# Moving transposes, casts and loads to DMA queues in a linear attention followed by a low-rank mixer

## The chip, the cores and the metric

One core of a Trainium2 chip runs the program. The metric is the device time of one execution in microseconds, the median of several. An engine has its own instruction queue: TensorE (PE), VectorE (DVE), ScalarE (ACT), GpSimd (POOL) and SyncE (SP, here only a queue for DMAs).

## What is computed

Batch 8, 8 heads, 576 positions, head size 64, so a model width of 512. From the reference, shortened:

```python
def phi(x): r = np.maximum(x, 0); return np.concatenate([r * cos_w, r * sin_w], axis=-1)   # 64 -> 128 features
kv = einsum('bhsf,bhsd->bhfd', phi(k), v);  z = phi(k).sum(axis=2)
x  = einsum('bhsf,bhfd->bhsd', phi(q), kv) / (einsum('bhsf,bhf->bhs', phi(q), z) + 1e-6)   # heads side by side: (B, S, 512)
u  = x + (x.transpose(0, 2, 1) @ U @ V).transpose(0, 2, 1)                                  # rank 32, over the positions
out = u + np.maximum(u @ w_ch1, 0) @ w_ch2                                                  # 512 -> 2048 -> 512
```

## The kernel before

A batch's 576 positions are four chunks of 128 (c = 0 to 3) and a tail of 64; the tails of an even and an odd batch share one tile of 128 rows. Attention of a batch: `k_prep` and `q_prep` (L221, L227) make the features in bf16, a cosine half and a sine half per chunk; `v_prep` (L195) casts v on GpSimd; `kv_unit` (L233) sums kv and z for four heads; the q features are transposed, by TensorE against an identity (`qtr_unit`, L254, copied out of PSUM), or by a DMA (`qtr_dma`, L268, used only where BY_DMA holds); `x_unit` (L333) makes one chunk of x. The first batch goes by halves of four heads (`den_unit`, `xh_unit`, L295, L312). Then `A_unit` (L360) makes U^T x, `u_unit` (L376) adds V^T A to one chunk, and u is transposed by `utr_unit` (L399) or `utr_dma` (L414). The first two batches get their transposed u straight from x and A (`uTd_open`, `uTd_close`, L427, L437).

The network runs on pairs of batches, in a list of 72 slots per pair (`mlp_slots`, L591): 16 main slots of the even batch (`g1_main`, L463: four matmuls of 128x512, emptied by ScalarE into `hid`), 16 of the odd one, 4 tail slots, and 36 slots of the second matmul (`g2_part`, four matmuls each; every fourth adds u on VectorE into `o_sb`, which SP stores). The order of all work is written by hand: instructions are issued in program order, and `todo` (L716 to L721) says behind which slot which unit of the next pair's attention stands. `pe_plan` (L554) and `prep_plan` (L581) give the offsets. BY_DMA (L534) is False, so all transposes are TensorE's.

Loads: all of them on SP's queue, but the tails of batch 0, U and V, which ScalarE issues (L126 to L138). The weights come as fp32 into a staging tile with two buffers (`w1_load`, L89), and GpSimd casts them (`w1_cast`, L97). A tile that is asked for again waits until its last reader is done; the number of buffers is `bufs`.

Of the kernel before, what the change touches and what calls it, by code (L numbers as in the profile page):

```python
# [17 lines left out]
def kernel(  # L18
# [13 lines left out]
    B = 8  # L32
# [56 lines left out]
    def w1_load(n):  # L89
        st = pool.tile([P, 4, 512], FP32, tag="wst", bufs=2, name="wst")  # L90
        nc.sync.dma_start(
            out=st,
            in_=moe_w_ch1.rearrange("(d p) n -> p d n", p=P)[:, :, n * 512 : n * 512 + 512],
        )
        return st

    def w1_cast(n, st, eng):  # L97
        cast(eng, w1_bf[:, :, n * 512 : n * 512 + 512], st)

    def w2_load(n):  # L100
        st = pool.tile([P, 4, 512], FP32, tag="wst", bufs=2, name="wst")
        nc.sync.dma_start(
            out=st,
            in_=moe_w_ch2.rearrange("(j p) n -> p j n", p=P)[:, n * 4 : n * 4 + 4, :],
        )
        return st

    def w2_cast(n, st, eng):
        cast(eng, w2_bf[:, n * 4 : n * 4 + 4, :], st)
# [16 lines left out]
    load_tail(kt[0], k, 0, A_)  # L126
    load_tail(qt[0], q, 0, A_)
    load_tail(vt[0], v, 0, A_)
    for h0 in (0, 4):
        load_main(kst[0], k, 0, h0, h0 + 4)  # L130
        load_main(qst[0], q, 0, h0, h0 + 4)
        load_main(vst[0], v, 0, h0, h0 + 4)
    A_.dma_start(
        out=stU[:, 0:4, :], in_=moe_U[0:512, :].rearrange("(p c) r -> p c r", c=4)
    )
    for lo in (0, TS):
        A_.dma_start(out=stU[lo : lo + TS, 4, :], in_=moe_U[512:S, :])
    A_.dma_start(out=stV, in_=moe_V)  # L138

# [19 lines left out]
    make_identity(nc, ident)  # L159

# [17 lines left out]
    G_.memset(U_bf, 0.0)  # L178
    G_.memset(V_bf, 0.0)
# [115 lines left out]
    def den_unit(b, hg, tag, bufs):  # L295
        d_ps = ps.tile([P, 5, 4], FP32, tag=tag, bufs=bufs, name="d_ps")
        for c in range(5):
            for i in range(4):
                h = hg * 4 + i
                nc.tensor.matmul(  # L300
                    out=d_ps[:, c, i : i + 1],
                    lhsT=qT_of(b, c, h),
                    rhs=kv_sb[b][:, h, D:E],
                    start=True,
                    stop=True,
                )
        rec = pool.tile([P, 5, 4], FP32, tag="rec5", bufs=2, name="rec5")
# [4 lines left out]
    def xh_unit(b, c, hg, rec, tag, bufs):  # L312
        x_alloc(b)
        rows = slice(0, P) if c < 4 else tail(b)
        acc = ps.tile([P, 4, D], FP32, tag=tag, bufs=bufs, name="xh_ps")
        for i in range(4):
            h = hg * 4 + i
            nc.tensor.matmul(
                out=acc[:, i, :], lhsT=qT_of(b, c, h), rhs=kv_sb[b][:, h, 0:D],
                start=True, stop=True,  # L320
            )
        nc.vector.tensor_tensor(
            out=x_of(b, c, rows)[:, hg * 256 : hg * 256 + 256].rearrange(
                "p (i d) -> p i d", d=D
            ),
            in0=acc[rows],
            in1=rec[rows, c, :].unsqueeze(2).to_broadcast(
                [P if c < 4 else TS, 4, D]
            ),
# [224 lines left out]
    def pe_plan(b):  # L554

        plan = []
        if BY_DMA:
            plan.append((-4, lambda: qtr_dma(b, 4, 5)))
            plan.append((-2, lambda: qtr_dma(b, 0, 2)))
            plan.append((0, lambda: qtr_dma(b, 2, 4)))  # L560
        else:
            for c in range(5):
                plan.append((2 * c, lambda c=c: qtr_unit(b, c)))
        for hg in range(2):
            plan.append((1 + 2 * hg, lambda hg=hg: kv_unit(b, hg, "X", 1)))
        for c in range(5):
            plan.append((5 + 2 * c + (2 if c == 4 else 0), lambda c=c: x_unit(b, c, "X", 1)))
        tx = "T" if BY_DMA else "X"
        plan.append((18, lambda: A_unit(b, tx, 1)))
        for n, c in enumerate((4, 0, 1, 2, 3)):  # L570
            plan.append((21 + 2 * n, lambda c=c: u_unit(b, c, tx, 1)))
            if not BY_DMA and c < 4:
                plan.append((24 + 2 * n, lambda c=c: utr_unit(b, c)))
        if b % 2 == 1:
            plan.append((23, lambda: utr_dma(b, 4, 5) if BY_DMA else utr_unit(b, 4)))
        if BY_DMA:
            plan.append((27, lambda: utr_dma(b, 0, 2)))
            plan.append((31, lambda: utr_dma(b, 2, 4)))
        return plan

    def prep_plan(b):  # L581

        plan = [(0, lambda: v_prep(b))]
        for n, c in enumerate((4, 0, 1, 2, 3)):
            plan.append((n, lambda c=c: k_prep(b, c, (V_, V_))))
            for i in range(2):
                engs = (A_, None) if i == 0 else (None, A_)
                plan.append(((n if BY_DMA else 3 + 2 * n) + i, lambda c=c, e=engs: q_prep(b, c, e)))
        return plan

    def mlp_slots(pr):  # L591
        e, o = 2 * pr, 2 * pr + 1
        slots = [lambda j=j: g1_main(e, j) for j in range(NJ)]
        slots += [lambda j=j: g1_main(o, j) for j in range(NJ)]
        slots += [lambda j=j: g1_tail(pr, j) for j in range(4)]
        slots += [
            lambda cc=cc, p=p: g2_part(pr, cc, p) for cc in range(9) for p in range(4)
        ]
        return slots
# [48 lines left out]
    w2st = {0: w2_load(0), 1: w2_load(1)}


    first = {}

    def at(j, *thunks):
        first.setdefault(j, []).extend(thunks)

    for n, c in enumerate(ORD):
        at(n // 2, lambda c=c: k_prep(1, c, (V_, A_)))
        at(4 + n // 2, lambda c=c: q_prep(1, c, (V_, A_)))
    for n, c in enumerate(ORD):
        at(1 + n // 2, lambda c=c: u_unit(0, c, "o", 2))  # L660
    for n, c in enumerate(ORD):
# [90 lines left out]
```

## Time and profile before

| | |
|---|---|
| median of 3 runs | 375.38 us (375.27 to 375.92) |
| profiled execution | 376.63 us, its span 374.5 us |
| mean granted TensorE clock | 0.991 |
| busy: TensorE, VectorE, ScalarE, GpSimd | 332.6, 180.9, 147.9, 44.5 us |
| moved by DMA | 46.68 MB, mean 125 GB/s |

The profile is one execution. Busy time of TensorE is modelled: a matmul's duration reaches into its neighbours', so its pace is read from start to start. In a row, "<-" in brackets names what ended the idle time before it.

### The profile page before, as it was taken

How to read it: one execution, taken by the hardware profiler on the slowest of the kernel's cores; microseconds unless marked ns; L12 is line 12 of the kernel's file. 1: busy time of each engine (PE TensorE's matmuls, PEld its weight loads, DVE VectorE, ACT ScalarE, POOL GpSimd, SP SyncE). 2: the span in 40 equal slices, each digit the busy share in tenths (PEclk: the TensorE clock that was granted, in tenths of full speed). 3: DMA queues.
4: the chain of work that ended last, by engine and by line, in shares of the span. 5: the costliest groups of instructions: out<-in, count | busy, mean ns of one | idle time of the engine just before them, and what ended most of it. 6: DMA issues, size and time to landing. Idle time of an engine off the chain costs nothing.

```text
span 374.5 us, 6199 instructions
## 1 busy us (share of the span) xinstructions
PE 332.6 (89%) x2589; PEld 183.1 (49%) x2589; DVE 180.9 (48%) x389; ACT 147.9 (39%) x254; POOL 44.5 (12%) x70
## 2 busy tenths in 40 slices
PE   0358787999989899999989999999899999999995
PEld 0356244446635534654755445544665444455442
DVE  3273865483676696543647483534565450000221
ACT  0861681369620420455671502455730006662000
POOL 2443642340000203030000003000000000000000
PEclk9999898999999999999999999999999999999999
DMA  8999889900329559900005278000012110000212
GB/s 210 308 299 329 290 279 283 291 17 16 114 77 292 152 163 291 275 19 2 0 30 169 72 229 263 2 0 2 0 39 76 56 58 28 0 2 28 86 56 84
DMA packets 47531, 46.68 MB, mean 125 GB/s; under 512 B 14064, under 2 KB 38768, under 8 KB 47504
## 3 DMA queue, kind: packets, MB, share of 16 engines
q1 hardware_dynamic: 45568, 45.75, 41.3%
q10 hardware_dynamic: 1936, 0.55, 0.7%
q8 instruction: 20, 0.33, 0.4%
q14 instruction: 7, 0.06, 0.0%
HBM read 36.86 MB, written 9.44 MB: 124 GB/s over the span
## 4 chain that ended last, share of the span: by engine, by line
PE 73%; DVE 14%; ACT 5%; issue 3%; DMA 3%; POOL 1%; ACTq 1%; POOLq 0%; DVEq 0%
PE o_ps L511 27%; PE g_ps L468 26%; PE t_ps L258 4%; DVE k_p L209 4%; PE kv_ps L241 3%; PE gt_ps L486 3%; DMA st_uv<-in_moe_U_dram 3%; PE x_ps L340 3%; PE a_ps L366 2%; ACT q_p L207 2%; PE va_ps L383 2%; DVE o_sb L522 2%; DVE u_bf L384 1%; PE t_ps L409 1%; DVE x_bf L350 1%
## 5 line engine op out<-in xcount | busy, mean ns | idle before, releaser
L475 ACT ACTIVATE hid<-g_ps 128x512 bf16<-128x512 f32 x128 | 76.3, 596 | 128.6 <-PE g_ps L468 128.6
L468 PE MATMUL g_ps<-uT,w_bf 128*128 128x512 bf16 x512 | 123.9, 385 | 0.1
L511 PE MATMUL o_ps<-w_bf,hid 128*128 128x512 bf16 x512 | 121.4, 379 | 0.0
L468 PEld LDWEIGHTS <-w_bf 128*128 128x128 bf16 x512 | 48.4, 99 | 53.7 <-issue 5.0
L511 PEld LDWEIGHTS <-hid 128*128 128x128 bf16 x512 | 47.7, 98 | 51.7 <-issue 2.9
L522 DVE TENSOR_TENSOR o_sb<-u_bf,o_ps 128x512 f32<-128x512 bf16 x32 | 21.9, 684 | 65.4 <-PE o_ps L511 65.1
L199 POOL CAST v_ext<-vst 128x512 bf16<-128x512 f32 (+1 forms) x36 | 19.2, 575 | 154.8 <-DMA vst<-in_v_dram 132.2
L115 DVE COPY q_pT<-t_ps 128x1024 bf16<-128x1024 bf16 x26 | 17.9, 689 | 20.4 <-PE t_ps L258 20.4
L384 DVE TENSOR_TENSOR u_bf<-x_bf,va_ps 128x512 bf16<-128x512 bf16 x32 | 21.7, 681 | 12.1 <-PE va_ps L383 11.9
L258 PE MATMUL t_ps<-ident,q_p 128*128 128x128 bf16 x256 | 21.0, 230 | 3.9 <-ACT q_p L207 3.3
L258 PEld LDWEIGHTS <-q_p 128*128 128x128 bf16 x256 | 17.7, 103 | 11.5 <-ACT q_p L207 5.6
L207 ACT ACTIVATE q_p<-qst,sinw 128x512 bf16<-128x512 f32 (+1 forms) x36 | 23.2, 662 | 0.0
L258 PE MATMUL t_ps<-ident,q_tl 128*128 128x128 bf16 x64 | 5.5, 229 | 18.8 <-ACT q_tl L207 15.1
L350 DVE TENSOR_TENSOR x_bf<-x_ps,rec 128x512 bf16<-128x512 f32 x28 | 19.4, 691 | 1.0
L383 PE MATMUL va_ps<-A_sb,V_bf 128*128 128x512 bf16 x40 | 15.2, 384 | 4.5 <-DVE u_bf L384 2.3
L209 DVE TENSOR_SCALAR k_p<-kst,cosw 128x512 bf16<-128x512 f32 (+1 forms) x36 | 18.8, 539 | 0.1
L207 ACT ACTIVATE q_p<-qst,cosw 128x512 bf16<-128x512 f32 x24 | 17.0, 710 | 1.5 <-DMA qst<-in_q_dram 1.4
L207 ACT ACTIVATE q_tl<-qt,cosw 64x512 bf16<-64x512 f32 x6 | 4.3, 717 | 32.7 <-PE t_ps L258 22.1
L115 POOL CAST w_bf<-wst 128x2048 bf16<-128x2048 f32 x8 | 15.5, 1934 | 14.4 <-DMA wst<-in_moe_w_ch_dram 14.4
L292 DVE TENSOR_SCALAR rec<-x_ps 128x8 f32<-128x8 f32 (+1 forms) x35 | 5.8, 165 | 20.9 <-PE x_ps L340 20.7
L340 PEld LDWEIGHTS <-q_pT 128*128 128x128 bf16 x224 | 10.5, 100 | 10.2 <-DVE x_bf L350 4.0
L486 PE MATMUL gt_ps<-uT_tl,w_bf 128*128 128x128 bf16 x256 | 15.4, 219 | 0.0
(88 smaller groups left out, 294.6 us busy)
## 6 DMA issues: line engine op xcount, KB each, us to landing
wst<-in_moe_w_ch_dram SPq DMA_DIRECT2D x8, 1024.0 KB, 6.9
out_dram<-o_sb SPq DMA_DIRECT2D x32, 256.0 KB, 2.4
kst<-in_k_dram SPq DMA_DIRECT2D x7, 1024.0 KB, 9.2
qst<-in_q_dram SPq DMA_DIRECT2D x7, 1024.0 KB, 7.2
vst<-in_v_dram SPq DMA_DIRECT2D x7, 1024.0 KB, 9.2
kst<-in_k_dram SPq DMA_DIRECT2D x2, 512.0 KB, 7.9
qst<-in_q_dram SPq DMA_DIRECT2D x2, 512.0 KB, 6.6
vst<-in_v_dram SPq DMA_DIRECT2D x2, 512.0 KB, 6.4
```

Source lines behind the costliest of these rows:

```text
L115: eng.tensor_copy(out=o, in_=i)
L207: nc.scalar.activation(out=o, in_=i, func=AF.Relu, bias=0.0, scale=w)
L209: eng.tensor_scalar(out=o, in0=i, scalar1=0.0, scalar2=w, op0=ALU.max, op1=ALU.mult)
L258: nc.tensor.transpose(out=t_ps[:, h, :], in_=q_p[b][:, c, h, :] if c < 4 else q_tl[:, h, :], identity=ident,)
L350: nc.vector.tensor_tensor(out=x_of(b, c, rows).rearrange("p (g i d) -> p g i d", g=2, d=D), in0=view[:, :, :, 0:D], in1=rec[rows].unsqueez ...
L383: nc.tensor.matmul(out=va, lhsT=V_bf[:, c, :], rhs=A_sb[b], start=True, stop=True)
L384: nc.vector.tensor_tensor(out=u_bf[b][:, c, :] if c < 4 else u_tl[b // 2][rows, :], in0=x_of(b, c, rows), in1=va[rows, :], op=ALU.add,)
L468: nc.tensor.matmul(out=g_ps.rearrange("p (c t) -> p c t", c=4), lhsT=w1_bf[:, d, j * P : j * P + P], rhs=uT[b][:, :, d, :], start=(d == 0) ...
L475: nc.scalar.activation(out=hid[b][:, j, :], in_=g_ps, func=AF.Relu, bias=0.0, scale=1.0)
L486: nc.tensor.matmul(out=g_ps[:, jj, :], lhsT=w1_bf[:, d, j * P : j * P + P], rhs=uT_tl[pr][:, d, :], start=(d == 0), stop=(d == 3),)
L511: nc.tensor.matmul(out=o, lhsT=lhs[:, j, c * P : c * P + P], rhs=w2_bf[:, j, :], start=(j == 0), stop=(j == NJ - 1),)
L522: nc.vector.tensor_tensor(out=o_sb, in0=u, in1=o, op=ALU.add)
```

## The change

- Weights: `w1_load` and `w2_load` become DMAs on GpSimd's queue that read fp32 and write bf16; the staging tiles and GpSimd's casts go. The eight are issued in the start, five of them behind `v_prep(1)`.
- Loads: batch 0 (without tails) and batch 1 stay on SP; the tails of batch 0, U and V, and all loads of batches 2 to 7 go to GpSimd's queue. ScalarE issues no DMA.
- For batches 2 to 7 the q features and u are transposed by DMAs on SP (one for the tail, two for two chunks each); `attention_plan` takes the place of `pe_plan` and `prep_plan`, over one list of 288 slots. Batch b starts at w = 34, 50, 106, 122, 178, 194; batch 2's and 3's network starts at slots 72 and 88, and so on.
- `qst`, `qt` and `x_bf` get a second buffer. Batch 1 uses `den_unit` and `xh_unit` over eight heads; the u units of batch 0 move behind slot 17; the order of the start changes.

The core of the diff:

```diff
     def w1_load(n):
-        st = pool.tile([P, 4, 512], FP32, tag="wst", bufs=2, name="wst")
-        nc.sync.dma_start(
-            out=st,
...
+        cs = slice(n * 512, n * 512 + 512)
+        nc.gpsimd.dma_start(
+            out=w1_bf[:, :, cs], in_=moe_w_ch1.rearrange("(d p) n -> p d n", p=P)[:, :, cs]
+        )
...
-    load_tail(kt[0], k, 0, A_)
...
+    load_tail(kt[0], k, 0, G_)
...
-    BY_DMA = False
...
+    def attention_plan(b):
+        plan = [(-6, lambda: v_prep(b))]
+        for n, c in enumerate(ORD):
+            plan.append((-6 + n, lambda c=c: k_prep(b, c, (V_, V_))))
+            plan.append((-6 + n, lambda c=c: q_prep(b, c, (A_, None))))
+            plan.append((-5 + n, lambda c=c: q_prep(b, c, (None, A_))))
+        plan.append((-3, lambda: qtr_dma(b, 4, 5)))
+        plan.append((-1, lambda: qtr_dma(b, 0, 2)))
+        plan.append((1, lambda: qtr_dma(b, 2, 4)))
+        plan.append((0, lambda: kv_unit(b, 0, "T", 1)))
+        plan.append((2, lambda: kv_unit(b, 1, "T", 1)))
+        for n, c in enumerate(ORD):
+            plan.append((6 + 2 * n, lambda c=c: x_unit(b, c, "X", 1)))
+        plan.append((16, lambda: A_unit(b, "T", 1)))
+        for n, c in enumerate(ORD):
+            plan.append((18 + 2 * n, lambda c=c: u_unit(b, c, "T", 1)))
         if b % 2 == 1:
+            plan.append((20, lambda: utr_dma(b, 4, 5)))
+        plan.append((24, lambda: utr_dma(b, 0, 2)))
+        plan.append((28, lambda: utr_dma(b, 2, 4)))
+        if b + 1 < B:
+            for at, t in zip((-5, -2, 2), loads(b + 1, G_)):
+                plan.append((at, t))
         return plan
...
+    v_prep(0, 4, 8, ORD, (G_, A_, G_, A_, G_))
+    w1_load(0)
+    w1_load(1)
+    l1[1]()
...
+    for n in range(4):
+        w2_load(n)
```

ORD is (4, 0, 1, 2, 3), 4 the tail; V_, A_ and G_ are VectorE, ScalarE and GpSimd.

## Rows read from the trace of the kernel before

**Rows 1.** The page: its busy times, and the chain that ended last by engine.
```profile
PE 332.6 (89%) x2589; PEld 183.1 (49%) x2589; DVE 180.9 (48%) x389; ACT 147.9 (39%) x254; POOL 44.5 (12%) x70
...
PE 73%; DVE 14%; ACT 5%; issue 3%; DMA 3%; POOL 1%; ACTq 1%; POOLq 0%; DVEq 0%
```

**Rows 2.** Windows: stage, its length, busy us (instructions) per engine, TensorE clock, DMA, GB/s.
```profile
12.10:38.20 26.10, 17.13 (x191) 13.91 (x192) 13.28 (x42) 14.15 (x33) 12.53 (x24) 1.00 1.04 317
38.20:75.10 36.90, 30.00 (x236) 15.41 (x235) 23.48 (x41) 19.06 (x32) 14.24 (x11) 0.91 0.97 284
75.10:147.90 72.80, 66.41 (x565) 36.59 (x564) 49.94 (x108) 29.19 (x49) 9.40 (x15) 1.00 0.48 134
147.90:228.30 80.40, 78.41 (x636) 43.55 (x634) 43.85 (x94) 34.28 (x56) 4.61 (x9) 1.00 0.40 115
228.30:308.10 79.80, 78.28 (x634) 43.57 (x633) 40.45 (x84) 27.94 (x46) 1.46 (x3) 1.00 0.14 44
```

**Rows 3.** Timeline of TensorE in pair 1: start, us, instruction.
```profile
148.78 0.61 PE L258 MATMUL t_ps<-ident,q_p 128*128 128x128 bf16 x8
149.23 1.03 PE L468 MATMUL g_ps<-uT,w_bf 128*128 128x512 bf16 x4
150.09 0.28 PE L241 MATMUL kv_ps<-v_ext,k_p 128*128 128x65 bf16 x4
...
150.70 1.03 PE L468 MATMUL g_ps<-uT,w_bf 128*128 128x512 bf16 x4
...
155.65 0.42 PE L340 MATMUL x_ps<-kv,q_pT 128*128 128x65 bf16 x8
155.91 1.02 PE L468 MATMUL g_ps<-uT,w_bf 128*128 128x512 bf16 x4
```

**Rows 4.** Groups by form in 228 to 308 us: busy, mean ns, idle time before.
```profile
L258 PE MATMUL t_ps<-ident,q_p 128*128 128x128 bf16 x64 | 4.9, 219 | 1.5 <-ACT q_p L207 1.5
```

**Rows 5.** Timeline of ScalarE in pair 0.
```profile
83.01 0.71 ACT L207 ACTIVATE q_tl<-qt,sinw 64x512 bf16<-64x512 f32 x1
83.62 0.58 ACT L475 ACTIVATE hid<-g_ps 128x512 bf16<-128x512 f32 x1
84.10 0.71 ACT L207 ACTIVATE q_p<-qst,cosw 128x512 bf16<-128x512 f32 x1
```

**Rows 6.** Timeline of the start, all engines.
```profile
0.73 0.44 SPq L75 DMA_DIRECT2D kst<-in_k_dram  x1
...
10.37 1.28 ACT L155 ACT_TABLE_LOAD   x1 [10.37 <-DMA qt<-in_q_dram]
...
12.36 1.18 DVE L209 TENSOR_SCALAR k_p<-kst,cosw 128x256 bf16<-128x256 f32 x4
...
19.74 1.96 POOL L115 CAST w_bf<-wst 128x2048 bf16<-128x2048 f32 x1
...
19.86 2.77 DVE L209 TENSOR_SCALAR k_p<-kst,cosw 128x256 bf16<-128x256 f32 x4
```

**Rows 7.** Line 209 on VectorE in 38 to 76 us: ns min, median, max.
```profile
L209 DVE TENSOR_SCALAR k_p<-kst,cosw x4: 471/484/2119, 40.2 to 44.2; 128x512 bf16<-128x512 f32 x4
```

**Rows 8.** DMA issues, us to landing: first 13 us; last two lines 148 to 228.
```profile
kst<-in_k_dram SPq DMA_DIRECT2D x2, 512.0 KB, 7.9
qst<-in_q_dram SPq DMA_DIRECT2D x2, 512.0 KB, 6.6
vst<-in_v_dram SPq DMA_DIRECT2D x2, 512.0 KB, 6.4
wst<-in_moe_w_ch_dram SPq DMA_DIRECT2D x1, 1024.0 KB, 6.9
...
st_uv<-in_moe_U_dram ACTq DMA_DIRECT2D x1, 64.0 KB, 10.1
...
out_dram<-o_sb SPq DMA_DIRECT2D x7, 256.0 KB, 2.3
kt<-in_k_dram SPq DMA_DIRECT2D x2, 128.0 KB, 5.0
```

More of the change, by code (lines that the diff above doesn't have):

```diff
@@ L125 @@
     alloc_v(0)
-    load_tail(kt[0], k, 0, A_)
[L127 to L138, printed above, removed]
     iota = const.tile([P, 5], FP32)
@@ L149 @@
         )
+    for h0 in (0, 4):
+        load_main(kst[0], k, 0, h0, h0 + 4)
+        load_main(qst[0], q, 0, h0, h0 + 4)
+        load_main(vst[0], v, 0, h0, h0 + 4)
+    load_tail(kt[0], k, 0, G_)
+    load_tail(qt[0], q, 0, G_)
+    load_tail(vt[0], v, 0, G_)
     halfpi = const.tile([P, 1], FP32)
@@ L159 @@
     make_identity(nc, ident)
+    G_.dma_start(
+        out=stU[:, 0:4, :], in_=moe_U[0:512, :].rearrange("(p c) r -> p c r", c=4)
+    )
+    for lo in (0, TS):
+        G_.dma_start(out=stU[lo : lo + TS, 4, :], in_=moe_U[512:S, :])
+    G_.dma_start(out=stV, in_=moe_V)
     k_tl = const.tile([P, H, 2 * D], BF16)
@@ L193, with v_prep @@
     u_bf, u_tl, uT, uT_tl = {}, {}, {}, {}
-    def v_prep(b, h0=0, h1=H, cs=range(5)):
+    def v_prep(b, h0=0, h1=H, cs=range(5), engs=None):
         vx = v_ext[b % 2]
-        for c in cs:
+        for n, c in enumerate(cs):
+            eng = engs[n] if engs else G_
             if c < 4:
-                nc.gpsimd.tensor_copy(out=vx[:, c, h0:h1, 0:D], in_=vst[b][:, h0:h1, c, :])
+                cast(eng, vx[:, c, h0:h1, 0:D], vst[b][:, h0:h1, c, :])
             else:
-                nc.gpsimd.tensor_copy(
-                    out=vx[tail(b), 4, h0:h1, 0:D], in_=vt[b][tail(b), h0:h1, :]
-                )
+                cast(eng, vx[tail(b), 4, h0:h1, 0:D], vt[b][tail(b), h0:h1, :])
     def scaled_relu(eng, o, i, w):
@@ L293, in recip, with den_unit @@
         nc.vector.reciprocal(out=rec, in_=rec)
-    def den_unit(b, hg, tag, bufs):
-        d_ps = ps.tile([P, 5, 4], FP32, tag=tag, bufs=bufs, name="d_ps")
+    def den_unit(b, h0, h1, tag, bufs):
+        n = h1 - h0
+        d_ps = ps.tile([P, 5, n], FP32, tag=tag, bufs=bufs, name="d_ps")
         for c in range(5):
-            for i in range(4):
-                h = hg * 4 + i
+            for h in range(h0, h1):
                 nc.tensor.matmul(
-                    out=d_ps[:, c, i : i + 1],
+                    out=d_ps[:, c, h - h0 : h - h0 + 1],
                     lhsT=qT_of(b, c, h),
@@ L310, in den_unit, with xh_unit @@
         return rec
-    def xh_unit(b, c, hg, rec, tag, bufs):
+    def xh_unit(b, c, h0, h1, rec, tag, bufs):
         x_alloc(b)
+        n = h1 - h0
         rows = slice(0, P) if c < 4 else tail(b)
-        acc = ps.tile([P, 4, D], FP32, tag=tag, bufs=bufs, name="xh_ps")
-        for i in range(4):
-            h = hg * 4 + i
+        acc = ps.tile([P, n, D], FP32, tag=tag, bufs=bufs, name="xh_ps")
+        for h in range(h0, h1):
             nc.tensor.matmul(
-                out=acc[:, i, :], lhsT=qT_of(b, c, h), rhs=kv_sb[b][:, h, 0:D],
+                out=acc[:, h - h0, :], lhsT=qT_of(b, c, h), rhs=kv_sb[b][:, h, 0:D],
                 start=True, stop=True,
@@ L548, in qq @@
             alloc_q(b)
-            load_tail(qt[b], q, b)
-            load_main(qst[b], q, b)
+            load_tail(qt[b], q, b, eng)
+            load_main(qst[b], q, b, eng=eng)
         return kk, vv, qq
[L554 to L573, printed above, removed]
-        if b % 2 == 1:
[L575 to L578, printed above, removed]
-        return plan
@@ L581, in prep_plan @@
[L581 to L599, printed above, removed]
@@ L630 @@
     a0 = A_unit(0, "X", 1, A_, 0, 256)
-    for c in ORD:
-        xh_unit(0, c, 1, rec1, "o", 2)
+    for c in ORD[:4]:
+        xh_unit(0, c, 4, 8, rec1, "o", 2)
     for d in range(2):
@@ L653, in at @@
+    for n in range(4):
+        w2_load(n)
+    beside = {}
     def at(j, *thunks):
-        first.setdefault(j, []).extend(thunks)
+        beside.setdefault(j, []).extend(thunks)
     for n, c in enumerate(ORD):
[L657 to L661, printed above, removed]
+        at((0, 0, 1, 1, 2)[n], lambda c=c: k_prep(1, c, (V_, A_)))
+        at((3, 4, 5, 6, 7)[n], lambda c=c: q_prep(1, c, (V_, A_)))
@@ new lines @@
+    at(13, lambda: A_unit(1, "T", 1))
+    at(13, lambda: uTd_close(1, 0, V_), lambda: uTd_close(1, 1, V_))
+    at(14, lambda: uTd_open(1, 2, "o", 2), lambda: uTd_open(1, 3, "X", 1))
+    at(14, lambda: uTd_close(1, 2, V_), lambda: uTd_close(1, 3, V_))
+    slots, todo = [], {}
+    for pr in range(NPAIR):
+        e, o = 2 * pr, 2 * pr + 1
+        slots += [lambda j=j, e=e: g1_main(e, j) for j in range(NJ)]
+        slots += [lambda j=j, o=o: g1_main(o, j) for j in range(NJ)]
+        slots += [lambda j=j, pr=pr: g1_tail(pr, j) for j in range(4)]
+        slots += [
+            lambda cc=cc, p=p, pr=pr: g2_part(pr, cc, p) for cc in range(9) for p in range(4)
+        ]
@@ new lines, with put @@
+    for j, ts_ in beside.items():
+        todo[j] = list(ts_)
+    def put(at, thunk):
+        todo.setdefault(at, []).append(thunk)
+    put(17, lambda: uTt_direct(0, "o", 2, V_))
+    for n, (b, c) in enumerate([(b, c) for b in range(2) for c in ORD]):
+        put(18 + n, lambda b=b, c=c: u_unit(b, c, "T", 1))
+    for n, t in enumerate(loads(2, G_)):
+        put(16 + n, t)
+    for b, w in ((2, 34), (3, 50), (4, 106), (5, 122), (6, 178), (7, 194)):
+        for o, t in attention_plan(b):
+            put(w + o, t)
@@ L725 @@
+    for i, s in enumerate(slots):
+        s()
+        for t in todo.get(i, []):
+            t()
 _INS = ['q', 'k', 'v', 'moe_U', 'moe_V', 'moe_w_ch1', 'moe_w_ch2']
```

145 lines of the change are left out of this document (42 added, 103 removed).

## The prediction

> **What bounds the kernel now.** I read the page first: TensorE is busy 89% of the span, and the chain of work that ended last lies on it for 73% [rows 1]. That is a mean over unlike stages, so I cut the span where the work changes [rows 2]: behind the wait for the first data (12.1 us) come the attention of batch 0 (to 38.2), the 16 main slots of batch 0 with the attention of batch 1 woven in (to 75.1), the rest of pair 0 (to 147.9), pairs 1 and 2; pair 3 has no attention beside it. Pairs 1 and 2 leave TensorE idle for 2.0 and 1.5 us of 80: there, what leaves TensorE leaves the time. The start and slots 0 to 15 are different: 17 us busy of 26 and 30 of 37, so waits for VectorE, ScalarE and data set the end. Next I read the pace of TensorE, from one start to the next, since a matmul's own duration overlaps its neighbour [rows 3]: a slot of four matmuls takes 0.86 us, eight transposes of q features 0.45, a kv unit 0.61, an x unit 0.26. From these follow the units not shown: four transposes of u take half of eight, 0.22; a u unit is one 512-wide matmul, 0.86 / 4 = 0.215; an A unit five, 1.08.
>
> **Transposes leave TensorE.** Batches 2 to 7 have five q units (0.45) each, and per pair nine u units (0.22): 10 x 0.45 + 9 x 0.22 = 6.5 us per pair, of three pairs 19.5 us. Their copies on VectorE go too; it is busy for 44 and 40 us of these 80, no bound, so nothing is counted for them.
> In pairs 1 and 2 all of the 6.5 us is on the path. The one wait of weight there, 1.5 us for the q features [rows 4], gets a successor: q features of an even batch are now made in the last four main slots and in the tail slots, where ScalarE also empties every slot. Its pace was 0.61 us for a feature half and 0.48 for a slot [rows 5]; two halves and a slot make 1.7 us against 0.86 of TensorE, over eight slots ScalarE needs 8 x 0.48 + 10 x 0.61 = 9.9 us, TensorE 7.0, and three buffers hide about 1.5 of the 2.9. So 1.4 replaces 1.5: **-6.5 for pair 1, -6.5 for pair 2**.
> In pair 0 behind slot 15 the window is 72.8 us with TensorE busy for 66.4 [rows 2]. Minus 6.5; five more u units come here from the slots before, +1.1; of the 6.4 idle, much is transposes, copies and x units queued on VectorE, and I leave 2.5 of it: -3.9. **-9.3**. Pair 3 has no attention: 0.
>
> **The start.** ScalarE issues seven DMAs and is held at them: its table load begins at 10.37 us and VectorE's main features, which need cosw, start at 12.36 [rows 6]. Without issues the table is there at about 3 us, and the data are late next: the first half of k, issued at 0.73, with the median of 7.9 us to land of such halves [rows 6, 8], is there at 8.6: -3.7. On the second half, four VectorE features took 2.77 us beside a weight cast on GpSimd and 1.18 without [rows 6]; those casts are gone: -1.6. Two half-size casts of v move to ScalarE, between half and the whole of 0.61 each: +1.0. **-4.3**. The tails now go through GpSimd's queue and k's is used first; no DMA of that queue is in the trace. From one side it is as quick as a store (2.3 us), from the other as slow as U in this stage, 10.1 [rows 8]: issued at about 1.3 us, it is there between 3.6 and 11.4. With the 8.6 of k as the later one, the wait shrinks by 1 to 3.7 us.
>
> **Slots 0 to 15.** Now 36.9 us. The weight casts go, beside which VectorE features of 0.48 us took up to 2.12 [rows 7]; the u units move behind. To slot 8 ScalarE is the longest: 9 x 0.48 + 10 feature halves x 0.61 [rows 5] + 3 copies of two slots' size, 3 x 0.96 = 13.3. Then TensorE: 7 slots x 0.86 + kv 1.2 + 40 narrow denominator matmuls at the kv unit's 0.61 / 20 (1.2) + x 1.3 + A 1.1 + four uT groups at 0.22 + 0.215 (1.7) = 12.5, and nothing covers the last A copy and four uT copies on VectorE, taken as 0.8 of a slot each: 3.5. Together 29.3, say 29.6: **-7.3**. Bounds: 0 (the same chain in a new order) and -12 (TensorE's work alone).
>
> **Weights and loads on GpSimd's queue.** Nothing of a casting DMA is in the trace. Lower bound: the weight load's 6.9 us per MB [rows 8], eight in some 55 us; upper: double. The first is needed at 34 us, the last four at some 85 (34 + 30 + 20 slots). Counted at 0: that cover is about 30 us long, if queue and cast keep the pace of SP. Loads on GpSimd stand behind five casts of v and go out 8 slots or more before their use; this cover is thinnest for q between an even and an odd batch. On SP an issue took 0.44 us [rows 6]; on GpSimd I bound it from above by the length of a weight cast there, 1.96 [rows 6]: six issues a batch and five casts of v (counted like a feature half, 0.6) then take 15 us of the 15 that 16 slots last, just full. Counted at 0.
>
> **DMA transposes.** No such transfer is in the trace. Per batch: one of 128 KB, two of 512 KB for q features; two of 256 KB for u (and per pair one tail); all on SP, where the output stores queue behind one that waits. Stores have three buffers, 12 slots, as cover. The x unit of chunk 2 runs 13 slots behind the first large one's place: 13 x 0.86 + kv 1.2 + three x units 0.8 = 13.2 us. For u the slack is 10 slots, 8.6 us, for 256 KB. From below, 256 KB in 2.3 us (the stores), so 4.6 per 512 KB; from above, rows cut into short pieces, as U's 64 KB in 128-byte pieces, 10.1 us, or kt's 128 KB in 256-byte pieces, 5.0 us, that is 20 per 512 KB [rows 8]. I take the halves of k, q and v, the same 512 KB in 1 KB pieces beside other loads: 7.9, 6.6 and 6.4, mean 7.0. Two behind one another: 14.0 against 13.2, a stall of 0.8 us in each of six batches: **+4.8**.
> [...]
>
> **Sum.** -4.3 - 7.3 - 9.3 - 6.5 - 6.5 + 4.8 = -29.1 us. The profiled execution took 376.63 us (span 374.5 and 2.1 around it), the median of the runs is 375.38, 1.25 less: 375.4 - 29.1 = 346.3, say **346.5 us**.
>
> **Rivals.**
> *Slow transposes (ends slower).* If 512 KB hold the queue for t us, each of six batches stalls 2t - 13.2. The other gains are 33.9 us, so the turning point is t = 9.4. At the pace of kt, t = 20: 6 x 26.8 = 161, less 33.9: about 502 us; at t = 10.5 it is 388. For it: features are read across partitions, unlike any row here, and the loads of the next batch go out in the same slots, 3.4 MB that at 284 GB/s [rows 2] fill the DMA engines for 12 us. Against it: each partition's row is long (4 KB), and the DMA engines are used for only 0.40 and 0.14 of pairs 1 and 2 [rows 2]. Chance 0.16. [...]
> *Late weights (ends slower).* If casting DMAs take twice 6.9 us, eight need 110 us from about 17 on, and the second half of the network, due at 85, stands some 40 us: 346 + 40 = 386. For it: VectorE and GpSimd do get into each other's way [rows 7]. Against it: GpSimd is busy for 1.5 to 14.2 us of a stage [rows 2], and its weight casts go. Chance 0.04. [...]
> *Only the transposes pay.* The start and slots 0 to 15 keep their time because the new queue feeds them no faster: 346.5 + 4.3 + 7.3 = 358. Chance 0.22; with stalls of 2 us rather than 0.8 per batch it reaches 365, inside the same case.
> *Everything hides.* No stall at the transposes, and the bounds of the start reached: 337 to 340. Chance 0.10.
>
> **How the numbers follow.** Forecast (340 to 353) 0.46, everything hides 0.10, only the transposes pay 0.22: faster 0.78. No change (0.2% is 0.75 us, about what a measurement of this kernel can tell) needs the gains to be just eaten: 0.02. Slower 0.20. The range runs from 338, just above the best case, to 380: it takes in the forecast, the smaller gain and stalls up to t near 9.8, and leaves out the far ends of the slower cases and of the best. The faster cases' own range is 338 to 366.
>
> **What would show it.** Right: pairs 1 and 2 at about 74 us each, with no transposes on TensorE; each x unit for chunks 0 and 2 waiting under 1 us for its transpose; the first feature before 9 us and the first main slot near 34; slots 0 to 15 in about 30. Wrong: DMA transposes longer than 9.4 us per 512 KB, read as TensorE's waits in front of the x units; main slots that wait for a weight DMA; features that wait for GpSimd's loads; output stores late behind SP's waits.

## The result and the profile after

The changed kernel takes **362.97 us** (median of 4 runs, 361.68 to 366.36) against 375.65 us (4 runs, 375.27 to 377.04) for the kernel before on the same chip: ratio 0.967, 95% interval 0.960 to 0.974. It is faster, by 12.7 us, where 29 were forecast. The profiled execution took 362.37 us, its span 360.6.

The page of the changed kernel, answering to [rows 1] (busy times; its GpSimd queue with packets, MB and share of 16 engines; the chain by engine):

```profile
PE 316.4 (88%) x2281; PEld 164.8 (46%) x2281; DVE 148.1 (41%) x328; ACT 146.5 (41%) x256; POOL 66.8 (19%) x109
...
q0 software_dynamic: 10256, 25.98, 28.0%
...
PE 65%; DMA 14%; ACT 9%; DVE 8%; issue 2%; POOL 0%; SPq 0%; ACTq 0%; DVEq 0%; POOLq 0%
```

TensorE lost 308 matmul instructions and 16 us of busy time, but DMA rose from 3% to 14% of the chain. Where that is, the windows of the same kernel by stage tell (columns as in [rows 2]; start, slots 0 to 15, rest of pair 0, pairs 1 and 2):

```profile
0.00:31.40 31.40, 16.03 (x190) 13.03 (x191) 16.16 (x55) 16.43 (x38) 13.58 (x34) 1.00 1.05 251
31.40:63.50 32.10, 25.69 (x250) 14.16 (x249) 14.95 (x29) 18.17 (x29) 10.70 (x15) 0.95 0.95 192
63.50:136.50 73.00, 64.21 (x473) 32.72 (x472) 40.06 (x83) 24.17 (x41) 27.04 (x38) 0.95 0.88 230
136.50:217.40 80.90, 74.56 (x518) 37.52 (x517) 34.11 (x75) 33.12 (x56) 15.47 (x22) 0.98 0.65 162
217.40:293.20 75.80, 72.76 (x517) 36.93 (x516) 33.84 (x75) 33.12 (x56) 0.00 (x0) 1.00 0.36 79
```

In pair 1 TensorE is now idle for 6.3 us of 80.9 and GpSimd works in the stage (its loads); in pair 2, with the same attention but no GpSimd instruction, it is idle for 3.0 of 75.8. Transposes left both stages; only pair 2 became shorter, by 4.0 us. What TensorE waited for behind slot 15, in the list of waits (us in total, times, longest; a larger row, 13.7 us for ScalarE's q features, lies in the start and in slots 0 to 15):

```profile
PE x_ps L324 <- DMA q_pT<-q_p: 9.8, 3, 5.2
PE kv_ps L229 <- DVE A_sb L105: 2.4, 3, 0.8
PE kv_ps L229 <- DVE u_tl L368: 2.3, 3, 0.8
PE gt_ps L470 <- ACT hid L459: 2.0, 3, 0.7
```

The first line replaces the 1.5 us of [rows 4]: x units stand for a transpose by DMA in batches 2, 3 and 5. The longest, on TensorE's timeline:

```profile
95.13 1.89 PE L495 MATMUL o_ps<-w_bf,hid 128*128 128x512 bf16 x8
102.17 0.62 PE L324 MATMUL x_ps<-kv,q_pT 128*128 128x65 bf16 x8 [5.16 <-DMA q_pT<-q_p]
102.60 3.60 PE L495 MATMUL o_ps<-w_bf,hid 128*128 128x512 bf16 x8
106.00 0.65 PE L324 MATMUL x_ps<-kv,q_pT 128*128 128x65 bf16 x8
```

The eight matmuls before the wait go from 95.13 to the wait's start in 1.9 us; the eight behind it need 3.4 (102.60 to 106.00). Windows around it (the number before the last two is the granted clock) say why: at the end of the wait TensorE is granted 0.50; it works at that level past 104 us and has 1.00 back at 108.

```profile
101.00:102.00 1.00, 0.00 (x0) 0.00 (x0) 0.00 (x0) 0.00 (x0) 0.14 (x1) 0.50 1.22 354
104.00:106.00 2.00, 2.00 (x7) 0.62 (x6) 2.00 (x5) 2.00 (x5) 0.00 (x0) 0.50 0.05 14
108.00:110.00 2.00, 1.97 (x10) 0.69 (x7) 0.60 (x2) 0.00 (x0) 1.10 (x2) 1.00 0.84 157
```

The timelines of SP and GpSimd show what went out together. SP issues batch 2's transposes; GpSimd's loads of batch 4, written for later slots, follow as soon as GpSimd is through with its casts of v and their buffers are free:

```profile
83.97 5.45 SPq L259 DMA_TRANSPOSE q_pT<-q_p  x2
...
190.86 10.55 SPq L259 DMA_TRANSPOSE q_pT<-q_p  x1
```

```profile
85.83 0.90 POOL L75 DMA_DIRECT2D kst<-in_k_dram  x1 [0.35 <-DVE kv L105]
87.40 0.89 POOL L75 DMA_DIRECT2D vst<-in_v_dram  x1
88.96 0.89 POOL L75 DMA_DIRECT2D qst<-in_q_dram  x1
```

The same happens at 190.86 (a single issue takes SP 10.55 us there). From issue to landing, by the view of the tile and by the list of DMAs (median us):

```profile
DMA to landing us min/median/max: 4.3/5.7/15.0
```

```profile
q_pT<-q_p SPq DMA_TRANSPOSE x12, 5.7
uT<-u_bf SPq DMA_TRANSPOSE x12, 3.1
w_bf<-in_moe_w_ch_dram POOLq DMA_DIRECT2D x8, 512.0 KB, 11.0
qst<-in_q_dram POOLq DMA_DIRECT2D x6, 1024.0 KB, 12.6
```

### The profile page after: what moved, and what is told of

Its sections match the earlier page's. It is cut to its first block, busy times and chain, and to the rows that moved or that the text cites. A ratio compares the mean times of both kernels' runs of the same rounds, so it can differ in the third digit from the quotient of the medians.

```text
span 360.6 us, 5601 instructions
## 1 busy us (share of the span) xinstructions
PE 316.4 (88%) x2281; PEld 164.8 (46%) x2281; DVE 148.1 (41%) x328; ACT 146.5 (41%) x256; POOL 66.8 (19%) x109
## 3 DMA queue, kind: packets, MB, share of 16 engines
q1 hardware_dynamic: 55648, 26.75, 32.1%
## 4 chain that ended last, share of the span: by engine, by line
PE 65%; DMA 14%; ACT 9%; DVE 8%; issue 2%; POOL 0%; SPq 0%; ACTq 0%; DVEq 0%; POOLq 0%
PE g_ps L452 27%; PE o_ps L495 25%; DMA q_pT<-q_p 12%; ACT q_p L195 4%; DMA qt<-in_q_dram 2%; PE a_ps L350 2%; PE va_ps L367 2%; DVE k_p L197 2%; PE kv_ps L229 2%; PE gt_ps L470 2%; PE x_ps L324 2%; ACT hid L459 1%; PE t_ps L246 1%; ACT k_p L195 1%; DVE x_bf L310 1%
## 5 line engine op out<-in xcount | busy, mean ns | idle before, releaser
L452 PE MATMUL g_ps<-uT,w_bf 128*128 128x512 bf16 x512 | 117.7, 382 | 0.2
L452 PEld LDWEIGHTS <-w_bf 128*128 128x128 bf16 x512 | 49.9, 98 | 59.9 <-issue 3.5
L105 DVE CAST kv<-kv_ps 128x260 bf16<-128x260 f32 x16 | 6.8, 428 | 64.0 <-PE kv_ps L229 64.0
L324 PE MATMUL x_ps<-kv,q_pT 128*128 128x65 bf16 x192 | 10.8, 200 | 10.6 <-DMA q_pT<-q_p 9.8
L229 PE MATMUL kv_ps<-v_ext,k_p 128*128 128x65 bf16 x256 | 12.9, 199 | 4.9 <-DVE A_sb L105 2.4
L470 PEld LDWEIGHTS <-w_bf 128*128 128x128 bf16 x256 | 15.1, 98 | 4.0 <-issue 2.3
L334 DVE TENSOR_TENSOR x_bf<-x_ps,rec 128x512 bf16<-128x512 f32 x24 | 16.6, 691 | 0.8
L197 DVE TENSOR_SCALAR k_p<-kst,cosw 128x512 bf16<-128x512 f32 (+1 forms) x36 | 15.9, 462 | 1.7 <-DMA kst<-in_k_dram 1.5
L229 PEld LDWEIGHTS <-k_p 128*128 128x128 bf16 x256 | 11.8, 102 | 8.3 <-DVE A_sb L105 3.9
L495 PE MATMUL o_ps<-w_bf,hid_tl 128*128 128x512 bf16 x64 | 15.4, 379 | 0.0
L246 PE MATMUL t_ps<-ident,q_tl 128*128 128x128 bf16 x16 | 2.0, 276 | 13.7 <-ACT q_tl L195 13.7
```

The costliest lines, as they stand in the source:

```text
L105: eng.tensor_copy(out=o, in_=i)
L197: eng.tensor_scalar(out=o, in0=i, scalar1=0.0, scalar2=w, op0=ALU.max, op1=ALU.mult)
L229: nc.tensor.matmul(out=acc[:, i, :], lhsT=k_p[b][:, c, h, :] if c < 4 else k_tl[:, h, :], rhs=vx[:, c, h, :], start=(c == 0), stop=(c == 4),)
L324: nc.tensor.matmul(out=acc[:, g, i * E : i * E + E], lhsT=qT_of(b, c, h), rhs=kv_sb[b][:, h, :], start=True, stop=True,)
L452: nc.tensor.matmul(out=g_ps.rearrange("p (c t) -> p c t", c=4), lhsT=w1_bf[:, d, j * P : j * P + P], rhs=uT[b][:, :, d, :], start=(d == 0) ...
L470: nc.tensor.matmul(out=g_ps[:, jj, :], lhsT=w1_bf[:, d, j * P : j * P + P], rhs=uT_tl[pr][:, d, :], start=(d == 0), stop=(d == 3),)
```

## The experiments

Stages are cut at the starts of ScalarE's first emptied slot of each part (the `hid` rows), so they are comparable between kernels; spans in us.

| kernel | start | slots 0-15 | rest of pair 0 | pair 1 | pair 2 | pair 3 | span |
|---|---|---|---|---|---|---|---|
| before | 39.5 | 34.7 | 74.8 | 80.4 | 79.8 | 65.3 | 374.5 |
| after | 32.8 | 31.8 | 72.9 | 80.9 | 75.9 | 66.3 | 360.6 |
| e1, loads left out | 33.4 | 31.5 | 64.7 | 75.9 | 75.9 | 66.3 | 347.7 |
| e2, kv tag | 33.4 | 32.0 | 78.4 | 82.3 | 74.3 | 66.3 | 366.7 |
| e3, TensorE transposes | 31.7 | 31.7 | 73.0 | 84.4 | 84.2 | 67.5 | 372.7 |
| e4, before with DMA transposes | 40.0 | 34.6 | 75.8 | 84.6 | 83.4 | 65.2 | 383.6 |
| e5, loads moved | 33.5 | 31.5 | 64.7 | 75.9 | 75.9 | 66.5 | 348.0 |
| e6, e5 and kv tag | 33.0 | 31.9 | 63.1 | 74.3 | 74.3 | 66.5 | 343.0 |
| e7, e5 and q earlier | 32.7 | 27.8 | 64.7 | 75.9 | 75.9 | 66.5 | 343.5 |
| e8, before, ScalarE issues none | 37.7 | 32.5 | 74.4 | 80.4 | 79.8 | 65.4 | 370.1 |
| e9, loads on SP | 32.5 | 31.9 | 64.7 | 75.9 | 75.9 | 66.7 | 347.7 |
| e10, e6 and q earlier | 32.6 | 27.8 | 63.1 | 74.3 | 74.3 | 66.5 | 338.6 |
| e12, loads on ScalarE | 32.7 | 31.6 | 72.5 | 83.6 | 83.1 | 66.3 | 369.9 |
| e13, moved loads on ScalarE | 32.0 | 31.7 | 64.7 | 81.1 | 79.9 | 66.5 | 356.0 |

**Theory:** loads that run beside the DMA transposes slow them. **Rival:** the transposes are slow by themselves, or come too late in the list of slots.

### e1: without the loads of batches 4 to 7

```diff
+            if b >= 4:
+                kst[b], kt[b] = kst[b - 2], kt[b - 2]
+                return
```

(and the like for v and q)

> The changed kernel without the loads of batches 4 to 7 (all but v's tails): these batches read the staging tiles of batches 2 and 3 again, so the output is not the reference's. Collision theory (the DMA transposes of batches 2, 3 and 5 are late, up to 15 us, because GpSimd's queue sends the next loads in the same microseconds): the three waits of TensorE for q_pT (5.2, 1.4 and 3.3 us) and the two stretches at the halved clock behind them go, 12 to 14 us, so about 349 to 351 us, with every DMA transpose of 512 KB landing in 4 to 7 us. Rival (the transposes are slow by themselves, or are held on SP by the stores before them): they stay late and the time stays at 361 to 364.

Measured: 349.12 us (348.88 to 349.45), ratio to before 0.930 (0.925 to 0.934). No wait for q_pT, and

```profile
DMA to landing us min/median/max: 4.2/4.5/6.4
```

So the collisions cost 362.97 - 349.12 = 13.9 us, all of it in the rest of pair 0 and in pair 1: 9.8 of idle TensorE, and about 4 for the slow clock behind two of the waits (an estimate from the granted clock: 5.4 and 3.4 us of work at half speed). Without these loads 512 KB take 4.5 us in the median.

### e2: kv units in the other PSUM buffers

```diff
-        plan.append((0, lambda: kv_unit(b, 0, "T", 1)))
+        plan.append((0, lambda: kv_unit(b, 0, "X", 1)))
```

(and the second kv unit likewise; T and X are buffers of PSUM: the kv matmuls write them and VectorE's 16 casts read kv_ps out of them, 0.43 us each in the changed kernel)

> The changed kernel with the kv units of batches 2 to 7 in the PSUM buffer X in place of T. Theory: the kv units of the odd batch wait behind A and u units of the even batch for their VectorE copies, 0.79 and 0.77 us a pair, in three pairs: 4.7 us less, about 358; the two waits in front of the kv units are gone from the trace. Rival (these waits lie beside another that ends later, the transposes, which then start no later and are waited for instead): less than 1.5 us gained, above 361.

A miss: 367.12 us (364.88 to 368.51), ratio 0.977 (0.972 to 0.983), 4 us slower than the changed kernel, though the ranges of the two overlap. The kv waits went, and pair 2, which has no loads, gained 1.6 us; but with less slack ahead (the time between a transpose's issue and the x unit that needs it) TensorE waited longer still for the transposes, as the rival had it:

```profile
PE x_ps L324 <- DMA q_pT<-q_p: 19.3, 3, 7.0
```

### e3: TensorE's transposes in the changed kernel

```diff
-        plan.append((-3, lambda: qtr_dma(b, 4, 5)))
...
+        for c, o in zip(ORD, (-3, -1, 0, 1, 3)):
+            plan.append((o, lambda c=c: qtr_unit(b, c, eng=V_, tag="X")))
...
+        for c in range(4):
+            plan.append((23 + 2 * c, lambda c=c: utr_unit(b, c)))
```

> The changed kernel with TensorE's transposes in place of the DMA transposes for batches 2 to 7; casting weights, GpSimd's queue and the new order stay. Theory (the DMA transposes take 19.5 us of TensorE's work away and give 13 to 14 back as waits and low clock): 363 + 6 = 369, with pairs 1 and 2 near 80 us and no wait for q_pT. Rival (they give back more than they take): below 362. Second rival (they gain all they were meant to, and the loss is elsewhere): 382.

A miss, half way between the theory's 369 and the second rival's 382: 375.46 us (374.03 to 376.9, 10 runs), ratio 1.001 (0.998 to 1.003). The start and slots 0 to 15 keep their gain of 10.8 us (39.5 + 34.7 against 31.7 + 31.7), and pairs 1 and 2 lose 8.4 of it, pair 3 2.3: TensorE waits in the new order for VectorE between transposes.

```profile
PE t_ps L246 <- DVE x_bf L334: 6.6, 6, 2.5
PE x_ps L324 <- DVE q_tlT L105: 2.8, 3, 0.9
```

So in this order a pair's transposes by DMA are worth 84.4 - 75.9 = 8.5 us where nothing collides, 12.5 us in all as the change has it. Part of this is the run's own: its q transposes stand in the buffer X, which the x units use too, and the two rows come to 3.1 us a pair.

### e4: DMA transposes in the kernel before

```diff
-    BY_DMA = False
+    BY_DMA = True
```

> The kernel before with its flag BY_DMA set: the same DMA transposes alone, with all loads on SP's queue in front of and behind them and 2 to 3 slots less slack. Collision theory: loads and transposes stand in one queue, a transpose behind a 1 MB load waits 4 us and more and the slack is 6 to 9 us, so some stalls stay: 362 to 372, and the waits for q_pT are found where a load was issued just before. Rival (only GpSimd's queue, which runs ahead of the slots, makes the collisions): 19.5 less, about 356.

A miss: 384.91 us (383.69 to 385.43), ratio 1.025 (1.020 to 1.029). The transposes land soon after their issue, yet TensorE waits longer for them than in the changed kernel:

```profile
DMA to landing us min/median/max: 4.3/4.7/7.2
```

```profile
PE x_ps L340 <- DMA q_pT<-q_p: 24.1, 5, 8.1
```

They are issued too late. Batch 3's q features are ready at 104.2 us, but on SP its transposes stand behind stores, loads and a transpose of u; TensorE begins to wait at 119.8, before the first one of 512 KB goes out (timelines of SP and TensorE):

```profile
121.10 3.56 SPq L271 DMA_TRANSPOSE q_pT<-q_p  x1
...
126.67 0.62 PE L340 MATMUL x_ps<-kv,q_pT 128*128 128x65 bf16 x8 [6.89 <-DMA q_pT<-q_p]
```

So it goes with three of the four long waits. The theory's mechanism, one queue for loads and transposes, is among the causes, though the time is far above its 372; no run separates the place in the list from what stands ahead on SP. The change needs the slack too: at 4.7 us a transfer, a late issue costs more than the transposes save.

### e5: the loads out of the way of the transposes

```diff
-        if b + 1 < B:
+        if b == 2:
             for at, t in zip((-5, -2, 2), loads(b + 1, G_)):
...
+        ev, od = loads(2 * p + 2, nc.sync), loads(2 * p + 3, nc.sync)
+        v_odd = loads(2 * p + 3, G_)[1]
+        for at, t in zip((-7, -6, 7, 8, 9, 32), (ev[0], ev[1], ev[2], od[0], od[2], v_odd)):
+            put(72 * p + at, t)
```

> The changed kernel, complete, with the loads of batches 4 to 7 at other times: k and v of the even batch at slots -7 and -6 of its pair's predecessor, its q and the odd batch's k and q at slots 7 to 9, all on SP's queue (so that they go out in slot time, when no features are transposed); v of the odd batch stays on GpSimd's queue. Collision theory: what counts is that loads and transposes don't fall together, so nearly all of the 13.9 us of the run without loads comes back although every byte is loaded: 349 to 352, no wait for q_pT. Rival (the loads' bytes themselves cost that time, wherever they stand, since the DMA engines are short in all of pairs 0 and 1): above 357.

349.75 us (349.24 to 349.91), ratio 0.931 (0.926 to 0.936), no wait for q_pT: all of e1's gain, with every byte loaded.

```profile
DMA to landing us min/median/max: 4.3/4.5/5.4
```

### e9, e12, e13: which queue, and when

Three runs tell apart what "beside" is. First the loads at the changed kernel's own slots, on SP's queue:

```diff
-            for at, t in zip((-5, -2, 2), loads(b + 1, G_)):
+            for at, t in zip((-5, -2, 2), loads(b + 1, nc.sync)):
```

> The changed kernel with the loads of batches 3 to 7 at their written slots, but on SP's queue in place of GpSimd's. Theory (transposes suffer wherever loads stand in front of or beside them): on SP the k and v loads go out in slot time, just before the transposes, and those stand behind 2.3 MB: waits for q_pT in nearly every batch, 362 or more. Rival (only GpSimd's queue, running ahead of the slots, makes them collide): 350 to 353.

Theory missed: 349.92 us (349.42 to 350.43), ratio 0.930 (0.923 to 0.937), no wait for q_pT. Here the load of q that stands behind the transposes on SP is issued behind them, at 92.63 us, after SP is through with them (SP's timeline, last row). The first transpose of a batch, behind v's load, is slower for it, up to 9.5 us, but inside its slack:

```profile
82.52 0.57 SPq L75 DMA_DIRECT2D vst<-in_v_dram  x1
83.80 7.98 SPq L259 DMA_TRANSPOSE q_pT<-q_p  x2
...
92.63 0.58 SPq L75 DMA_DIRECT2D qst<-in_q_dram  x1
```

```profile
DMA to landing us min/median/max: 4.3/4.6/9.5
```

That left two readings: GpSimd runs ahead of the slots, or a second queue is enough. ScalarE keeps the slots' pace and has its own queue (in this run's page 17.70 MB go over q10, SP's 26.75 over q1; `nc.scalar` for `G_` in the same line):

> The changed kernel with the loads of batches 3 to 7 at the same written slots, issued by ScalarE instead of GpSimd. ScalarE reaches a slot when its own work there is done, so its queue keeps the pace of the slots, but its ring is another than SP's, on which the transposes go. Theory (what makes loads and transposes collide is that GpSimd reaches the issues long before their slots): about as with the loads on SP, 350 to 354 us, the q transposes landing in a median under 5 us with no wait of TensorE for q_pT, less some 0.6 us of ScalarE's time for each of 30 issues where ScalarE is close to setting the pace (the loads stand in tail slots of the even batches). Rival (two queues side by side share the DMA engines, whatever the slot): 358 to 364 us, landings of 6 us and more in the median, and waits for q_pT as in the changed kernel.

The theory missed again: 373.98 us (371.69 to 376.36, 10 runs), ratio 1.000 (0.997 to 1.003), slower even than the rival's figure. It is not that GpSimd runs ahead. Transposes and loads collide in all three pairs, because the loads now keep to their slots (GpSimd had sent batch 7's before pair 2 began):

```profile
DMA to landing us min/median/max: 4.4/8.9/14.6
```

```profile
PE x_ps L324 <- DMA q_pT<-q_p: 16.3, 4, 5.6
```

ScalarE's issues are not the cause here: TensorE waits for `hid` no longer than in the changed kernel, 2.0 us.

Last, e5's loads, which stand away from the q transposes, on ScalarE's queue:

```diff
+        ev, od = loads(2 * p + 2, nc.scalar), loads(2 * p + 3, nc.scalar)
```

> The kernel with the moved loads, its loads of batches 4 to 7 issued by ScalarE at the same slots (the odd batch's v stays on GpSimd, as there). No load then goes out in the 15 us ahead of a q transpose, but the loads have a queue of their own again. Theory (it is the time that loads and transposes spend on the DMA engines side by side from two queues; apart in time, a second queue does no harm): 349 to 352 us, pairs 1 and 2 at 76 us, q transposes landing in a median of 4.5 us, no wait of TensorE for q_pT. Rival (a second hardware queue with loads slows the transposes for good, or ScalarE's issues hold up its own work): pairs 1 and 2 over 79 us, 356 us and more.

360.76 us (357.74 to 363.24), ratio 0.964 (0.957 to 0.972): in time the rival's case, in mechanism each had half. No wait of TensorE for q_pT is left, so a second queue that is apart in time did little harm here: a median of 5.1 us, against 4.5 in e5 (not quite the 15 us of the expectation: some loads go out 8 us ahead of an odd batch's transposes, and GpSimd's load of v falls beside them; the slowest transpose of this run took 8.6 us, inside its slack). But the span is 8 us longer than e5's, in pairs 1 and 2, where TensorE waits for `hid`. On ScalarE's timeline the fifth and sixth load in a row take it 4 us to issue, and `hid` stands behind them (the same at 219.08):

```profile
138.04 2.25 ACTq L81 DMA_DIRECT2D qt<-in_q_dram  x1
140.38 1.72 ACTq L75 DMA_DIRECT2D qst<-in_q_dram  x1
142.14 2.31 ACT L459 ACTIVATE hid<-g_ps 128x512 bf16<-128x512 f32 x4 [3.59 <-issue]
```

```profile
PE g_ps L452 <- ACT hid L459: 6.9, 2, 3.7
```

So TensorE's waits for q_pT take both: loads on another queue than the transposes, and at the same time (9.8 us in the changed kernel and 16.3 in e12, none in e9 and e13). It is not only that SP is held at its issues: in the changed kernel SP was through with batch 2's at 89.4 us, and the wait for them ended at 102.2. A DMA transpose of 512 KB took 4.5 us in the median without such loads (e1, e5) and up to 15.0 beside them; by what mechanism, no row shows.

### e6, e7, e10, e11: what else the new order costs

e6 is e5 with e2's edit:

> The run with moved loads, with the kv units in the PSUM buffer X. Theory: the buffer change made the kernel slower only because each slot's time that it took away was slack of a late transpose; without collisions it gives 1.6 us a pair, 4.7 in all, below the run with moved loads: 345 to 347. Rival (the buffer X itself costs, its x units waiting for the kv copy): equal or slower.

344.89 us (344.19 to 345.0), ratio 0.918 (0.913 to 0.923): 4.9 us less, in all three pairs. Without collisions, kv units queued behind A's and u's buffers are worth the sum of their two rows of waits (2.4 + 2.3).

e7 is e5 with batch 1's q features earlier:

```diff
-at((3, 4, 5, 6, 7)[n], lambda c=c: q_prep(1, c, (V_, A_)))
+at((2, 2, 3, 4, 5)[n], lambda c=c: q_prep(1, c, (V_, A_)))
```

> The run with moved loads, with the q features of batch 1 at slots 2, 2, 3, 4, 5 in place of 3 to 7. Theory of slots 0 to 15 (32 us, forecast 29.6): VectorE stands idle for 6.9 us in front of a copy of transposed q, with q features queued behind it, and TensorE and ScalarE then wait for these in turn; earlier features give 2 to 3 us there and the same in the whole. Rival (ScalarE is simply full up to slot 9): less than 1 us.

345.71 us (345.36 to 346.34), ratio 0.921 (0.916 to 0.926): -4.0, more than the 2 to 3 expected, and slots 0 to 15 go from 31.5 to 27.8. Part of that may be the clock: from 40 to 42 us TensorE is granted 0.50 in the changed kernel, and the profiled executions' mean is 0.990 in e5 and 0.999 in e7. In the changed kernel VectorE stands 6.93 us before the copy of a transpose, with the next features queued behind it:

```profile
42.28 0.69 DVE L105 COPY q_pT<-t_ps 128x1024 bf16<-128x1024 bf16 x1 [6.93 <-PE t_ps L246]
42.88 1.65 DVE L197 TENSOR_SCALAR q_p<-qst,cosw 128x512 bf16<-128x512 f32 x2
```

e10 has all three edits:

> Moved loads, kv units in X, and batch 1's q features earlier, together. The three gains lie in different stages (loads and kv units in the pairs, q features in slots 0 to 15), so they add: 349.8 - 4.9 - 4.0 = 340.9. If one only moved a wait that the other had found: above 343.

**340.56 us** (340.35 to 342.13), ratio 0.906 (0.900 to 0.912): the gains add up, and it beats both kernels, the changed one by 22 us. e11 spreads the even batches' q features over twice the slots as well:

> The same with the q features of the even batches begun at slot -12 rather than -6, one half a slot. Theory: the waits of the tail slots for ScalarE, 0.65 us and some 0.3 a pair, go: 1 to 3 us less than without, 338 to 340. Rival (ScalarE's sum of work in those slots is the bound, not its order): same.

340.29 us (339.71 to 340.91), ratio 0.904 (0.899 to 0.910): no gain that can be told from e10, as the rival had it. The 2.0 us of waits in the tail slots are gone from the list, but the stages together gain only 0.6.

### e8: the kernel before, without DMA issues on ScalarE

```diff
-    load_tail(kt[0], k, 0, A_)
...
+    load_tail(kt[0], k, 0, G_)
```

(the other tails, U and V likewise)

> The kernel before with one part of the change: the tails of batch 0, U and V are loaded through GpSimd's queue behind the iotas, so ScalarE issues no DMA. Theory: the first features start near 7.5 us in place of 12.1, and the first main slot comes 3 to 5 us earlier, 371 us. Rival (the start of slots is set by the weights or by batch 1's loads, so what the features gain is waited for later): 375.

Between the two: 373.1 us (372.09 to 374.64, 10 runs), ratio 0.993 (0.990 to 0.996). The first feature comes 4.4 us earlier (12.09 to 7.69), the first main slot only 1.8: VectorE waits for kv, which waits for v, whose casts stand on GpSimd behind those of U and V. VectorE's and GpSimd's timelines:

```profile
7.69 0.34 DVE L208 TENSOR_SCALAR k_tl<-kt,cosw 64x256 bf16<-64x256 f32 x1 [3.23 <-DMA kt<-in_k_dram]
...
17.64 0.43 DVE L115 CAST kv<-kv_ps 128x260 bf16<-128x260 f32 x1 [5.78 <-PE kv_ps L240]
```

```profile
12.36 0.29 POOL L181 CAST U_bf<-st_uv 128x128 bf16<-128x128 f32 x1 [4.70 <-DMA st_uv<-in_moe_U_dram]
...
15.02 1.43 POOL L198 CAST v_ext<-vst 128x256 bf16<-128x256 f32 x4
```

In the changed kernel v's casts come first, part of them on ScalarE; without that order the freed queue brings the first main slot forward by 1.8 us, less than half of the 4.4. That slots 0 to 15 are 2.2 us shorter here too stays unexplained.

## Why the prediction was right in direction and wrong in size

Point by point, by the stage table (after less before):

- **The start**, forecast -4.3: -6.7 (-6.0 to -7.8 over the runs with this start). The first feature comes at 7.44 us, 4.6 earlier instead of 3.7. It waits for k's tail on GpSimd, which landed 5.9 us after its issue, at 7.3, in the middle of the bounds 3.6 and 11.4. The first half of k was not the later one: the forecast's 7.9 us is the median of two halves, and the first of them landed after 4.9 in the kernel before and after 4.0 here (the list of DMAs, last row). The four features of the second half took 1.31 us for the 2.77 of [rows 6].

```profile
7.44 0.35 DVE L197 TENSOR_SCALAR k_tl<-kt,cosw 64x256 bf16<-64x256 f32 x1 [2.24 <-DMA kt<-in_k_dram]
...
13.26 1.31 DVE L197 TENSOR_SCALAR k_p<-kst,cosw 128x256 bf16<-128x256 f32 x4 [1.54 <-DMA kst<-in_k_dram]
```

```profile
kst<-in_k_dram SPq DMA_DIRECT2D x1, 512.0 KB, 4.0
```

- **Slots 0 to 15**, forecast -7.3: -2.9. Two steps failed. The window of 36.9 us in [rows 2] ended at 75.1, where slot 18 begins (the rows below, of the kernel before: 16 matmuls are slots 14 to 17). The 16 slots had taken 34.7 to 35.0, so the step's own 29.6 us was a gain of 5.1 to 5.4. And it saw ScalarE and TensorE as the chain, not VectorE's queue held by a copy; e7 gives that 3.7 us back and beats the 29.6.

```profile
71.43 3.62 PE L468 MATMUL g_ps<-uT,w_bf 128*128 128x512 bf16 x16
...
75.10 1.03 PE L468 MATMUL g_ps<-uT,w_bf 128*128 128x512 bf16 x4
```

- **The transposes on TensorE**, forecast -9.3, -6.5, -6.5: without collisions (e5) -10.1, -4.5, -3.9. The 2.0 to 2.6 us that pairs 1 and 2 fall short are mostly the two kv waits, 1.6 a pair, an order that the prediction did not look at; e6 reaches -11.7, -6.1, -5.5. Pair 3, forecast 0, loses 1.0: three u units of the last batch moved into it, 0.65 us at the forecast's price; the rest stays open.
- **The stalls, forecast +4.8: +13.9. This is the step that failed.** It gave every transfer one pace, 7.0 us per 512 KB, so two of them 14.0 against a slack of 13.2: 0.8 us of stall in each of six batches, and nothing for the clock behind a wait. The slack was about right: 13.0 us in batch 2, from the issue of the first at 83.97 to the x unit's turn at 97.0. The pace was not. Measured are 4.5 us in the median where no loads of another queue run beside them (e1, e5), with no stall at all, and up to 15.0 beside GpSimd's loads, past the turning point of 9.4. The stall falls on batches 2, 3 and 5 alone, with 9.8 us of waits and about 4 of slow clock. The prediction had the loads in the same slots as an argument for its slow rival, but took its pace from loads beside one another on SP's queue, not from what a second queue sends beside a transpose. (U's 64 KB, one of its bounds from above, went in packets of 512 bytes, not 128: an estimate from the 1936 packets of ScalarE's queue in the kernel before, of which the tails take 1536 at 256 bytes and U's would take 512 at 128; the sum doesn't use it.)
  Of the prediction's two bounds the one from below, 4.6 us per 512 KB at the pace of the stores, came near the 4.5; u's transposes of 256 KB landed after 3.1 us in the median, a plain store of 256 KB after 2.3 [rows 8].
- **Weights and loads on GpSimd**, counted at 0: a casting DMA took 11.0 us in the median for 512 KB written, 1 MB read (between 6.9 and twice that), an issue 0.7 to 0.9 us; no main slot waited for a weight. The rival of late weights is out.

The sum without the stalls, -33.9, would nearly have met e6's span (343.0 against 374.5, -31.5). The changed kernel is not there mainly because of the stall term, 9 us too small, the kv waits (4.9 us in e6), and slots 0 to 15 (4.4), less what the start gave more (2.4). That the time still lies between 338 and 380 is owed to the room left there for smaller gains and longer stalls, not to the 4.8. The rival that only the transposes pay gave a time near the measured one by luck, for another reason than its own: start and slots 0 to 15 did pay.

## What to carry to other kernels

A transfer with a deadline belongs on a queue and into a stretch of time in which no second queue loads in bulk: price it with the loads that run beside it (here 512 KB took 4.5 us in the median without them and up to 15.0 with them), and move the loads (13 us here; more slack instead was not tried). Freeing an engine shifts the wait to the next queue (here q features stood behind a copy for which VectorE waited 6.93 us), so look at which buffer and which queued copy is late next; here these were worth 9 us more. The windows of a forecast should be cut at the slot where the work changes, found by counting that slot's rows.

## What had not been expected of the hardware

- In TensorE's wait of 5.2 us the granted clock fell to 0.50, and it was still there 2 to 4 us into the work behind it: this wait cost more than its length (eight matmuls 3.4 us, not 1.9). At the wait of 3.3 us in batch 5, which ends at 205.9, the clock is 1.00 at the end and 0.64 and 0.51 in the two windows of 2 us that follow, so there the fall shows only in the work.
- A DMA transpose of 512 KB between two on-chip tiles landed in 4.5 us in the median (e1, e5), about like a plain load of 512 KB at the very start (4.0), and quicker than such loads beside one another, 6.4 to 7.9 us [rows 8].
- An issue was not of fixed length: in e13 ScalarE's loads took it 0.6 us each until the fifth in a row, then 2.25; SP's transposes of 512 KB took it 1.3 to 3.1 us in e1 and, beside loads in the changed kernel, up to 10.55.
